# Sliding-window attention and two MLPs: S as an fp32 product of unsplit q and k

## The chip, the cores and the metric

The kernel runs on one core of a Trainium2 chip. The metric is the device time of one execution in microseconds; of the kernel before there are three, with a median of 708.91 us (707.36 to 709.56). The core has five engines with an instruction queue each, worked off in program order: PE (matmul), DVE, ACT, POOL and SP, which here only issues transfers.

## The reference

```python
def _attn_ref(q, k, v, n_global, n_local):       # 2 batches, 8 heads, 768 rows, 64 wide
    scores = (1 / np.sqrt(D)) * np.matmul(q, k.transpose(0, 1, 3, 2))
    keep = is_global | is_local                  # first 8 columns, or the last 96 positions
    bias = -slopes[:, None, None] * dist[None, :, :]
    scores = np.where(keep, scores + bias[None], -1e9)
    a = np.exp(scores - np.max(scores, axis=-1, keepdims=True))
    a = a / (np.sum(a, axis=-1, keepdims=True) + 1e-09)
    return np.matmul(a, v)
def _moe_ref(x, w_gate, w_val, w_out, rms_g):    # 1536 tokens, 512 wide, 1536 inside
    rms = np.sqrt(np.mean(x * x, axis=-1, keepdims=True) + 1e-06)
    xn = x / rms * rms_g
    g = xn @ w_gate
    return (g / (1 + np.exp(-g)) * (xn @ w_val)) @ w_out
def _moe2_ref(x, w_in, w_out, s, b):             # 2048 inside
    r = np.maximum(x @ w_in, 0.0)
    return (s * (r * r) + b) @ w_out
```

The output is `_moe2_ref(_moe_ref(attention))`. The weights come as 8-byte floats, q, k and v as fp32. The fast program, the one that runs here, covers the case of 8 global columns and 96 local ones.

## The kernel before, in words

The attention is cut into 12 units of 128 query rows: units 0 and 1 are the first rows of the two batches (128 key columns), units 2 to 6 and 7 to 11 the others (232 columns: 8 global ones, 96 earlier, 128 own). A unit is worked in two groups of four heads. For each group: the score products S on PE; the bias added and the minimum taken on DVE (`top`); exponentials on ACT; the sum inverted on DVE; the normalisation (`nrm`) on POOL or DVE; transposes P on PE; a copy from PSUM (`cp`); the product X with v on PE. After both groups the unit's RMS norm (`finish`): squares, their sum over 512 features, a mean through PE (L377), the root on POOL, a broadcast through PE (L388), a scaling, and the split of x into a high and a low half in the reduced format `float32r`.

Products of fp32 numbers in `float32r` are made in three terms (high x high, low x high, high x low). q and k are split for that too: `q_hi` and `k_hi` (a rounding copy on ACT or DVE, L759 and L761, L781 and L783) and `q_lo` and `k_lo` (a subtraction, L764 and L787). q is loaded into one raw buffer and k into another; the split writes into a persistent window of k (`kw`, three slots of 136 columns) and a pair of buffers of q.

Beside the attention run the first weights: 512 KB loads into three raw buffers, and seven steps of conversion from 8-byte floats into two halves (`conv`: ACT, four or five on DVE, POOL). Gate and value products of the first MLP are put between the attention's products as soon as their inputs are there (`gate`: 256 columns, three terms). The rest of both MLPs follows as a dense row of matmuls of 512 columns; two more conversions and loads run ahead of it all the time.

The order on every engine comes from `arrange`, a list scheduler that runs while the program is built. Each operation has a kind, a rank, durations on the engines that may do it, and resources (buffers) that it takes and gives back; `AHEAD` shifts the rank of a kind. A transfer counts there as an issue on SP plus a fixed delay. SP issues loads strictly in the order found; `lq`, `lk`, `lv` and `wload` are their kinds. PE gets idle matmuls (`warm`) in planned gaps of the first 40 us.

Of the kernel before, what the change touches and what calls it, by code (L numbers as in the profile page):

```python
# [8 lines left out]
F32 = mybir.dt.float32  # L9
# [31 lines left out]
    "P": -8.16, "S": -6.41, "X": 42.13, "bias": 20.72, "bias0": -89.67, "conv": 2.49, "cp": -19.31, "exp": -0.05,  # L41
    "fin": -19.74, "gate": -44.51, "inv": -11.3, "lk": -17.92, "lq": -12.18, "lv": -13.03, "mask": 103.87, "nrm": 110.41,
    "silu": -12.26, "split": -0.02, "top": -12.96, "wload": -16.57,
}
CONV = 1.65

SPARE = {"V": 0.95, "A": 0, "P": 0}
LOOK = {"V": 0.01, "A": 0.21, "P": 0.23, "T": 0}
KEEP = 3
COLD = 40.0  # L50
# [4 lines left out]
def kernel(  # L55
# [131 lines left out]
    class Mlp:  # L187
# [171 lines left out]
        def finish(self, nrm, xb, b, c0):  # L359
# [235 lines left out]

    class Op:
        def __init__(self, kind, rank, fn, on, after=(), take=(), give=()):
            self.kind, self.fn, self.on, self.after, self.take, self.give = kind, fn, on, after, take, give
            self.rank = rank + AHEAD.get(kind, 0.0)
            self.item = None  # L600
            self.start = self.end = self.eng = None


    def arrange(ops, size):
        free = dict.fromkeys("PVATS", 0.0)
# [3 lines left out]
        while left:  # L609
            cands = []  # L610
            for op in left:
# [19 lines left out]
                _, d, e, t = min((max(t, free[e]) + d + SPARE.get(e, 0.0), d, e, max(t, free[e])) for e, d in op.on.items())  # L631
                cands.append((t, op, d, e))
# [4 lines left out]
            free[e] = end  # L637
            for r in op.take:
                takes[r].append(op)
# [6 lines left out]
    def fast_program(fctx):  # L646
# [8 lines left out]
        in_p = pool("in_p", 1)  # L655
        v_p = pool("v_p", 2)
        qs_p = pool("qs_p", 2)
# [6 lines left out]
        size = {"xx": 1, "u": 2, "yy": 1, "w": 2, "qraw": 1, "kraw": 1, "v": 2, "qs": 2, "kw": 1, "kf": 1, "t": 3, "pt": 2}  # L664
# [3 lines left out]
        def op(kind, rank, fn, on, after=(), take=(), give=()):  # L668
            ops.append(Op(kind, rank, fn, on, after, take, give))
            return ops[-1]  # L670

# [5 lines left out]
        def bias_of(e, hs):  # L677
# [3 lines left out]
        bias0 = op("bias0", 0.6, bm0_half, {"V": 0.55})  # L681
        masked = op("mask", 3.0, lambda e: mask(D1, scr, PREV), {"V": 1.1})
        biases = [
            op("bias", 3.1 + g, lambda e, g=g: bias_of(e, range(4 * g, 4 * g + 4)), {"V": 0.8, "P": 3.6}, [masked]) for g in range(2)
# [4 lines left out]
        for n in range(RING):  # L689
            r = 3.0 + CONV * n  # L690
            if n < 3:
                loads[n] = op("wload", -3 + 0.1 * n, lambda e: mlp.load(), {"S": 0.9}, take=["raw"])
# [8 lines left out]
            lag = 2.5 if n else 4.0  # L701
            a = a0 = op("conv", r, begin, {"A": 0.7}, [(loads[n], lag)], ["cv"])
            for m, on in enumerate(({"V": 0.45}, {"V": 0.5}, {"V": 0.7}, {"V": 0.7}, {"A": 0.64}, {"V": 0.72, "P": 1.45}), 1):
                a = op("conv", r, lambda e, part=part, m=m: part[m](e), on, [a], give=[("raw", loads[n])] * (m == 4) + [("cv", a0)] * (m == 6))
                if m == 4 and n + 3 < RING:

                    loads[n + 3] = op("wload", r, lambda e: None, {"S": 0.9}, [a], ["raw"])
            convs.append(a)


        xs, kbuf, owner = [], {}, {}
        for n, (b, i) in enumerate(units):
# [5 lines left out]

            if n:

                def load_q(e, st=st, b=b, i=i):
                    st["q"] = in_p.tile([128, NPAIR, 128], F32, name="q", tag="q")
                    nc.sync.dma_start(st["q"], q[b, i])


                slot = 0 if i <= 1 else (i - 1) % 3 if b else i % 3
                if b == 0:
                    slot = i % 3
                fresh = not first and slot == 0
                kw_cols = 128 if first else WIN if fresh else KB  # L730

                def load_k(e, st=st, b=b, i=i, first=first, w=kw_cols):
                    kt = in_p.tile([128, NPAIR, WIN], F32, name="k", tag="k")
                    st["k"] = kt[:, :, WIN - w :]
                    if w == WIN:
                        nc.sync.dma_start(kt[:, :, :PREV], k[b, i - 1, :, :, KB - PREV :])
                    nc.sync.dma_start(kt[:, :, WIN - min(w, KB) :], k[b, i, :, :, GLOB * first :])

                lq = op("lq", r - 4, load_q, {"S": 0.45}, take=["qraw"])
                lk = op("lk", r - 4, load_k, {"S": 0.45}, take=["kraw"])  # L740
                lag = 2.2
            else:
                st["q"], st["k"] = q0, k0
                slot, fresh, kw_cols = 0, False, 128
                lq = lk = op("lq", -9, lambda e: None, {"S": 0.1}, take=["qraw", "kraw"])
                lag = 0.0
# [6 lines left out]
            lv = op("lv", r - 3.5, load_v, {"S": 0.6}, take=["v"])  # L753

            def q_hi(e, st=st):
                st["qh"] = qs_p.tile([128, NPAIR, 128], F32R, name="qhi", tag="qhi")
                st["ql"] = qs_p.tile([128, NPAIR, 128], F32R, name="qlo", tag="qlo")
                if e is V:
                    V.tensor_copy(st["qh"], st["q"])  # L759
                else:  # L760
                    A.activation(st["qh"], st["q"], AF.Copy)  # L761

            def q_lo(e, st=st):
                e.tensor_tensor(st["ql"], st["q"], st["qh"].bitcast(F32), op=ALU.subtract)  # L764

            def k_hi(e, st=st, n=n, b=b, i=i, slot=slot, fresh=fresh, w=kw_cols):
                first = i == 0
                if first and b:

                    kb = [bm_p.tile([128, NPAIR, 128], F32R, name=f"kf{m}") for m in range(2)]  # L770
                    st["w"] = kb
                    dst = kb
                else:
                    if first or fresh:
                        kbuf[b] = [bm_p.tile([128, NPAIR, PREV + 3 * KB], F32R, name=f"kw{m}", tag=f"kw{m}") for m in range(2)]
                    c1 = PREV + (slot + 1) * KB
                    dst = [t[:, :, c1 - w : c1] for t in kbuf[b]]
                    st["w"] = [t[:, :, c1 - (128 if first else WIN) : c1] for t in kbuf[b]]
                st["kd"] = dst
                if e is V:  # L780
                    V.tensor_copy(dst[0], st["k"])  # L781
                else:
                    A.activation(dst[0], st["k"], AF.Copy)  # L783

            def k_lo(e, st=st):
                hi, lo = st["kd"]
                e.tensor_tensor(lo, st["k"], hi.bitcast(F32), op=ALU.subtract)  # L787

            wide = NPAIR * kw_cols
            new = ["kf"] if first and b else ["kw"] if (first or fresh) else []  # L790
            qh = op("split", r - 1.5, q_hi, {"A": 0.63, "V": 0.5}, [(lq, lag)], ["qs"])
            ql = op("split", r - 1.5, q_lo, {"V": 0.72, "P": 1.35}, [qh], give=[("qraw", lq)])
            kh = op("split", r - 1.5, k_hi, {"A": 0.2 + 0.00084 * wide, "V": 0.2 + 0.0006 * wide}, [(lk, lag)], new)
            kl = op("split", r - 1.5, k_lo, {"V": 0.16 + 0.00105 * wide, "P": 0.9 + 0.0011 * wide}, [kh], give=[("kraw", lk)])
            if new:
                owner[new[0]] = kh
            own = "kf" if first and b else "kw"
            last_use = (first and b) or n + 1 == NU or (b == 0 and i in (2, 5)) or (b == 1 and i == 3)
            X = []
            for g in range(2):  # L800
# [344 lines left out]
```

## Time and profile before

| | |
|---|---|
| runs, median (range) | 708.91 us (707.36 to 709.56) |
| profiled execution | 707.75 us, span 706.0 us |
| PE busy | 663.3 us (94%) |
| DVE busy | 436.5 us (62%) |
| ACT busy | 286.2 us (41%) |
| POOL busy | 183.3 us (26%) |
| chain that ended last | PE 78%, DVE 9%, DMA 6% |

Shares over the whole span mix two parts. Up to some 162 us the attention runs and all engines take part; behind it PE is busy nearly throughout. The busy time of PE is made of overlapping matmuls, so it says less than the chain of waits, which gives each matmul only its place in the row. A wait that ends with a load of q is a stretch in which the chain's next instruction had nothing but that load to wait for.

### The profile page before, as it was taken

Reading aid. Unit: us, or ns where it says so; the run is one execution under the profiler, and the core shown is the slowest. Engines: PE = TensorE matmul, PEld = TensorE weight load, DVE = VectorE, ACT = ScalarE, POOL = GpSimd, SP = SyncE. Lnnn points to the kernel's source line nnn. Section 1 sums busy time; section 2 is a strip of 40 time slices with the busy share of each in tenths; the row PEclk is TensorE's granted clock in tenths of the full one; section 3 lists DMA queues with packets and bytes.
Section 4 is the critical chain, followed back from the end, with each engine's and each line's share of the span. In section 5 each row is a group of like instructions: output and inputs, shape, how many; then the busy total and the mean of one; then the engine's idle time right before and its main releaser. Section 6 shows DMA issues by size and latency. Waiting matters only on the chain.

```text
span 706.0 us, 9562 instructions
## 1 busy us (share of the span) xinstructions
PE 663.3 (94%) x3558; PEld 549.5 (78%) x3558; DVE 436.5 (62%) x879; ACT 286.2 (41%) x599; POOL 183.3 (26%) x153
## 2 busy tenths in 40 slices
PE   7667959899999999999999999999999997999996
PEld 5456858798888888888888887888888875888885
DVE  5877859963775555777532379766565699322322
ACT  3576748771332222334332335333333444322321
POOL 2467658751221111222200023221111124000000
PEclk9889889999999999999999999999999999999999
DMA  5444244400232222333300024222212233100101
GB/s 179 112 122 143 60 131 128 133 30 1 65 114 64 83 64 60 94 110 96 90 1 0 1 61 120 89 89 61 60 59 64 81 95 90 61 1 0 60 0 65
DMA packets 40334, 51.82 MB, mean 73 GB/s; under 512 B 4424, under 2 KB 31048, under 8 KB 40280
## 3 DMA queue, kind: packets, MB, share of 16 engines
q1 hardware_dynamic: 39608, 50.87, 24.2%
q8 instruction: 30, 0.49, 0.3%
q10 hardware_dynamic: 672, 0.26, 0.1%
q14 instruction: 24, 0.20, 0.1%
HBM read 47.98 MB, written 3.15 MB: 72 GB/s over the span
## 4 chain that ended last, share of the span: by engine, by line
PE 78%; DVE 9%; DMA 6%; ACT 2%; issue 2%; POOL 1%; SPq 1%; ACTq 0%; DVEq 0%; POOLq 0%
PE ps L182 24%; PE ps L184 24%; PE ps L183 24%; DMA q<-in_q_dram 5%; PE ps L884 2%; DVE u L269 2%; DVE u L275 2%; PE ps L810 1%; PE ps L865 1%; DVE t L823 1%; DVE u L272 1%; DMA words<-in_n_local_dram 1%; DVE sm L844 1%; DVE u L266 1%; ACT t L838 1%
## 5 line engine op out<-in xcount | busy, mean ns | idle before, releaser
L182 PE MATMUL ps<-xyh,hi_i 128*128 128x512 f32 x192 | 74.7, 389 | 0.0
L183 PE MATMUL ps<-xyl,hi_i 128*128 128x512 f32 x192 | 74.7, 389 | 0.0
L184 PE MATMUL ps<-xyh,lo_i 128*128 128x512 f32 x192 | 74.7, 389 | 0.0
L182 PE MATMUL ps<-xyh,hi_g 128*128 128x512 f32 (+1 forms) x176 | 63.0, 358 | 0.9 <-DVE p L949 0.9
L182 PE MATMUL ps<-xyh,hi_v 128*128 128x512 f32 (+1 forms) x176 | 63.3, 360 | 0.3 <-ACT ss L394 0.3
L523 DVE SCALAR_TENSOR_TENSOR gt<-side,sb 128x512 f32<-128x512 f32 x48 | 37.6, 784 | 39.7 <-ACT side L522 39.7
L183 PE MATMUL ps<-xyl,hi_v 128*128 128x512 f32 (+1 forms) x176 | 61.8, 351 | 0.0
L183 PE MATMUL ps<-xyl,hi_g 128*128 128x512 f32 (+1 forms) x176 | 61.7, 350 | 0.0
L184 PE MATMUL ps<-xyh,lo_v 128*128 128x512 f32 (+1 forms) x176 | 61.6, 350 | 0.0
L184 PE MATMUL ps<-xyh,lo_g 128*128 128x512 f32 (+1 forms) x176 | 61.6, 350 | 0.0
L522 ACT ACTIVATE side<-ps 128x512 f32<-128x512 f32 x48 | 28.7, 598 | 76.5 <-PE ps L184 76.5
L288 POOL TENSOR_TENSOR lo_i<-u,hi_i 128x512 fp32r<-128x512 f32 x16 | 23.3, 1455 | 138.9 <-ACT hi_i L284 137.5
L435 ACT ACTIVATE side<-ps 128x512 f32<-128x512 f32 (+1 forms) x32 | 18.3, 571 | 95.8 <-PE ps L184 95.8
L269 DVE TENSOR_SCALAR u<-u 128x512 int32<-128x512 int32 x68 | 51.2, 753 | 0.0
L838 ACT ACTIVATE t<-t,mn 128x232 f32<-128x232 f32 (+1 forms) x96 | 44.2, 463 | 15.9 <-DVE mn L823 15.9
L436 DVE SCALAR_TENSOR_TENSOR side<-side,ps 128x512 f32<-128x512 f32 (+1 forms) x32 | 20.9, 654 | 42.8 <-ACT side L435 42.8
L266 DVE TENSOR_SCALAR u<-u 128x512 f32<-128x512 f32 x68 | 40.2, 593 | 4.6 <-ACT u L262 4.5
L183 PEld LDWEIGHTS ps<-xyl,hi_i 128*128 128x128 f32 x192 | 36.0, 188 | 7.6
L184 PEld LDWEIGHTS ps<-xyh,lo_i 128*128 128x128 f32 x192 | 36.0, 188 | 7.5
L182 PEld LDWEIGHTS ps<-xyh,hi_i 128*128 128x128 f32 x192 | 36.0, 188 | 7.4
L884 PE MATMUL ps<-pt,vw 116*64 116x128 f32 (+1 forms) x352 | 27.2, 300 | 14.8 <-ACT pt L872 12.5
L288 POOL TENSOR_TENSOR lo_p<-u,hi_p 128x512 fp32r<-128x512 f32 x16 | 22.0, 1377 | 72.4 <-ACT hi_p L284 67.6
(155 smaller groups left out, 1654.7 us busy)
## 6 DMA issues: line engine op xcount, KB each, us to landing
raw_i<-in_moe_w_in_dram SPq DMA_DIRECT2D x16, 512.0 KB, 3.6
raw_p<-in_moe_w_out_dram SPq DMA_DIRECT2D x16, 512.0 KB, 3.6
raw_g<-in_moe_w_gate_dram SPq DMA_DIRECT2D x12, 512.0 KB, 3.6
raw_v<-in_moe_w_val_dram SPq DMA_DIRECT2D x12, 512.0 KB, 6.6
raw_o<-in_moe_w_out_dram SPq DMA_DIRECT2D x12, 512.0 KB, 3.4
vw<-in_v_dram SPq DMA_DIRECT2D x10, 464.0 KB
out_dram<-o SPq DMA_DIRECT2D x12, 256.0 KB, 2.9
q<-in_q_dram SPq DMA_DIRECT2D x11, 256.0 KB, 4.1
```

The lines of the kernel that those rows point to most:

```text
L182: T.matmul(out=o, lhsT=ahi, rhs=bhi, start=first, stop=False)
L183: T.matmul(out=o, lhsT=ahi, rhs=blo, start=False, stop=False)
L184: T.matmul(out=o, lhsT=alo, rhs=bhi, start=False, stop=last)
L266: e.tensor_scalar(u, u, 2.0**-15, None, op0=ALU.max)
L269: V.tensor_scalar(ui, ui, 5, 2, op0=ALU.logical_shift_left, op1=ALU.logical_shift_right)
L288: e.tensor_tensor(lo, u, hi.bitcast(F32), op=ALU.subtract)
L435: A.activation(th[:, :w], g, AF.Tanh, scale=0.5)
L436: V.scalar_tensor_tensor(th[:, :w], in0=th[:, :w], scalar=1.0, in1=g, op0=ALU.add, op1=ALU.mult)
L522: A.activation(r, o, AF.Relu)
L523: V.scalar_tensor_tensor(g, in0=r, scalar=s_col, in1=r, op0=ALU.mult, op1=ALU.mult)
L838: A.activation(t[:, hh, :], t[:, hh, :], AF.Exp, bias=mn[:, hh : hh + 1], scale=-1.0, accum_out=sm[:, hh : hh + 1])
L884: T.matmul(out=st["xb"][64 * j : 64 * j + 64, (2 * g + pp) * 128 : (2 * g + pp + 1) * 128], lhsT=st["v"][:kn, m, (4 * g + hh) * D : (4 * g ...
```

## The change

S is one fp32 product of q and k as they were loaded; the 24 splits of the units are gone, and the buffers for them. q is loaded into one of three buffers, k straight into its slot of the window, which is a resource of its own for the scheduler. The scheduler gets an engine `D` on which transfers take their size over 220 KB/us, and a port: an operation on POOL and one on DVE that is marked `port` do not overlap in the plan. In units 0 to 3 (`SUMMED`) the sum of squares over the four feature blocks is made by four products into one PSUM column, without the adds on POOL or DVE. The table `AHEAD`, `CONV`, `SPARE` and `LOOK` have new values. Of a gate and value pair both weights must be converted before the gate product starts.

```diff
 AHEAD = {
-    "P": -8.16, "S": -6.41, "X": 42.13, "bias": 20.72, "bias0": -89.67, "conv": 2.49, "cp": -19.31, "exp": -0.05,
+    "P": -44.35, "S": 19.7, "X": 23.57, "bias": 26.48, "bias0": -17.44, "conv": 1.04, "cp": -65.5, "exp": -1.83,
...
+RATE = 220.0
+SUMMED = 4
...
             def total(e):
                 part["R"] = ps("w")
-                T.matmul(out=part["R"][:, 128:129], lhsT=ss, rhs=ones, start=True, stop=True)
+                parts = [xn[:, kk] for kk in range(KD)] if summed else [ss]
+                for kk, x in enumerate(parts):
+                    T.matmul(out=part["R"][:, 128:129], lhsT=x, rhs=ones, start=kk == 0, stop=x is parts[-1])
...
+                for e, d in op.on.items():
+                    s = max(t, free[e])
+                    if e == "P" or e == "V" and op.port:
+                        s = max(s, port["V" if e == "P" else "P"])
+                    key = (s + d + SPARE.get(e, 0.0), d, e, s)
+                    best = key if best is None else min(best, key)
...
-        size = {"xx": 1, "u": 2, "yy": 1, "w": 2, "qraw": 1, "kraw": 1, "v": 2, "qs": 2, "kw": 1, "kf": 1, "t": 3, "pt": 2}
+        size = {"xx": 1, "u": 2, "yy": 1, "w": 2, "v": 2, "q": 3, "k0": 1, "k1": 1, "k2": 1, "kf": 1, "t": 3, "pt": 2}
...
+        def fetch(kind, rank, fn, kb, after=(), take=(), issue=0.45):
+            a = op(kind, rank, fn, {"S": issue}, after, take)
+            return a, (op(kind, rank, None, {"D": kb / RATE}, [a]), 1.8)
...
+            c1 = PREV + (slot + 1) * KB
+            st["k"] = k0 if n == 0 else kalone if first else kwin[:, :, c1 - WIN : c1]
+
+            def load_q(e, st=st, b=b, i=i):
+                st["q"] = qs_p.tile([128, NPAIR, 128], F32, name="q", tag="q")
+                nc.sync.dma_start(st["q"], q[b, i])
+
+            def load_k(e, st=st, b=b, i=i, first=first, fresh=fresh):
+                if fresh:
+                    nc.sync.dma_start(st["k"][:, :, :PREV], k[b, i - 1, :, :, KB - PREV :])
+                nc.sync.dma_start(st["k"][:, :, 0 if first else PREV :], k[b, i, :, :, GLOB * first :])
...
+                gone = ["kf"] if first else [f"k{m}" for m in range(3) if m == slot - 1 or m == slot and (m == 2 or i == NT - 1)]
+                gone = [("q", lq)] + [(x, user[x]) for x in gone]
...
-                        for m, (qq, kk) in enumerate((("qh", 0), ("ql", 0), ("qh", 1))):
-                            for j in range(2):
-                                T.matmul(
-                                    out=st["sc", g][:, j, pp, :],
-                                    lhsT=st[qq][64 * j : 64 * j + 64, pr, :],
-                                    rhs=st["w"][kk][64 * j : 64 * j + 64, pr, :],
-                                    start=m == 0,
-                                    stop=m == 2,
-                                )
+                        for j in range(2):
+                            T.matmul(
+                                out=st["sc", g][:, j, pp, :],
+                                lhsT=st["q"][64 * j : 64 * j + 64, pr, :],
+                                rhs=st["k"][64 * j : 64 * j + 64, pr, :],
+                                start=True,
+                                stop=True,
+                            )
...
-            a = ga = op("gate", rf, lambda e, p=product, st=st: p(e, st, "g", 0), {"T": 0.74}, xdep + [convs[2 * f]] + hold, ["w"])
+            a = ga = op("gate", rf, lambda e, p=product, st=st: p(e, st, "g", 0), {"T": 0.74}, xdep + [convs[2 * f], convs[2 * f + 1]] + hold, ["w"])
```

SP from the start of the fast program. Before: weights (`raw_g`, `raw_v`), then k, v and q of units 1 and 2.

```order
L237 DMA raw_g<-in_moe_w_gate_dram 128x4x256
L237 DMA raw_v<-in_moe_w_val_dram 128x4x256
L237 DMA raw_g<-in_moe_w_gate_dram 128x4x256
L737 DMA k<-in_k_dram 128x4x128
L751 DMA vw<-in_v_dram 128x512 x2
L723 DMA q<-in_q_dram 128x512
L737 DMA k<-in_k_dram 128x4x136
L723 DMA q<-in_q_dram 128x512
L737 DMA k<-in_k_dram 128x4x136
```

And now (`kf` is unit 1's k, `kw` the window):

```order
L770 DMA vw<-in_v_dram 128x512
L239 DMA raw_g<-in_moe_w_gate_dram 128x4x256
L239 DMA raw_v<-in_moe_w_val_dram 128x4x256
L239 DMA raw_g<-in_moe_w_gate_dram 128x4x256
L752 DMA kf<-in_k_dram 128x4x128
L747 DMA q<-in_q_dram 128x512
L770 DMA vw<-in_v_dram 128x512
L751 DMA kw<-in_k_dram 128x4x96
L752 DMA kw<-in_k_dram 128x4x136
L747 DMA q<-in_q_dram 128x512
L752 DMA kw<-in_k_dram 128x4x136
L747 DMA q<-in_q_dram 128x512
```

The v of unit 0 stands first, and the loads of q and k reach unit 3 before the first weight that must wait for a raw buffer; before, a weight and a v stood ahead of unit 3's q.

SP in the second half, where unit 7's window starts again in the first slot (the two `kw` rows of 96 and 136 columns). Before, from the k of unit 7 (L736, L737) on:

```order
L736 DMA k<-in_k_dram 128x4x96
L737 DMA k<-in_k_dram 128x4x136
L751 DMA vw<-in_v_dram 116x2x512
L237 DMA raw_g<-in_moe_w_gate_dram 128x4x256
L751 DMA vw<-in_v_dram 116x2x512
L723 DMA q<-in_q_dram 128x512
L737 DMA k<-in_k_dram 128x4x136
L723 DMA q<-in_q_dram 128x512
L237 DMA raw_v<-in_moe_w_val_dram 128x4x256
```

And now:

```order
L239 DMA raw_v<-in_moe_w_val_dram 128x4x256
L239 DMA raw_g<-in_moe_w_gate_dram 128x4x256
L239 DMA raw_v<-in_moe_w_val_dram 128x4x256
L770 DMA vw<-in_v_dram 116x2x512
L751 DMA kw<-in_k_dram 128x4x96
L752 DMA kw<-in_k_dram 128x4x136
L239 DMA raw_g<-in_moe_w_gate_dram 128x4x256
L752 DMA kw<-in_k_dram 128x4x136
L747 DMA q<-in_q_dram 128x512
```

The loads of k of unit 7 now stand behind three weights and a v, and q of units 7 and 8 is already ahead of them.

PE at unit 2, the first with 232 columns. Before, its second group: S in six rows of two matmuls (`qhi`, `qlo`; `kw_214` and `kw_215` are the halves of k), then transposes and X of earlier groups.

```order
L377 MATMUL ps_470<-ones,ss 128x1
L810 MATMUL ps_474<-kw_214,qhi 128x232 x2
L810 MATMUL ps_474<-kw_214,qlo 128x232 x2
L810 MATMUL ps_474<-kw_215,qhi 128x232 x2
L810 MATMUL ps_474<-kw_214,qhi 128x232 x2
L810 MATMUL ps_474<-kw_214,qlo 128x232 x2
L810 MATMUL ps_474<-kw_215,qhi 128x232 x2
L865 MATMUL ps_491<-ident,t 128x128 x4
L388 MATMUL ps_470<-ident,rstd 128x128
L884 MATMUL ps_513<-pt,vw 64x128 x4
L865 MATMUL ps_519<-ident,t 128x128 x4
```

And now, from its first group on:

```order
L783 MATMUL ps_418<-kw,q 128x232 x4
L835 MATMUL ps_424<-ident,t 128x128 x4
L176 MATMUL ps_446<-warm 128x512 x3
L854 MATMUL ps_450<-pt,vw 64x128 x4
L783 MATMUL ps_455<-kw,q 128x232 x4
L176 MATMUL ps_477<-warm 128x512 x5
L835 MATMUL ps_483<-ident,t 128x128 x4
L783 MATMUL ps_490<-kw,q 128x232 x4
L854 MATMUL ps_450<-pt,vw 64x128 x4
```

S is one row of four matmuls; the idle matmuls (`warm`) stand in other places.

## Rows read from the trace of the kernel before

**Rows 1.** Stretches: us, then PE, PEld, DVE, ACT, POOL busy, PEclk, DMA share, GB/s
```profile
8.00:162.20 154.20, 126.53 (x1155) 107.64 (x1156) 122.39 (x396) 100.88 (x291) 98.32 (x81) 0.90 0.39 115
162.20:706.00 543.80, 532.57 (x2395) 438.71 (x2393) 310.79 (x462) 183.48 (x306) 83.56 (x61) 1.00 0.21 62
```

**Rows 2.** Chain of waits to 165 us: start us, us, what
```profile
27.83 9.62 DMA q<-in_q_dram
57.84 7.01 DMA q<-in_q_dram
87.90 9.25 DMA q<-in_q_dram
127.42 4.12 DMA q<-in_q_dram
162.02 0.22 PE ps L388 x2
```

**Rows 3.** Stretches: sum over the four waits of rows 2; then 110 to 140
```profile
sum 30.00, PE 19.60 PEld 16.42 DVE 20.73 ACT 10.40 POOL 16.73; mean PE 4.90 PEld 4.11 DVE 5.18 ACT 2.60 POOL 4.18
110.00:140.00 30.00, 27.23 (x290) 24.55 (x290) 29.37 (x89) 24.34 (x68) 24.24 (x21) 1.00 0.46 143
```

**Rows 4.** Timeline of SyncE, 78 to 88 us: start, us, what
```profile
78.45 0.28 SPq L751 DMA_DIRECT2D vw<-in_v_dram  x1
86.91 0.39 SPq L237 DMA_DIRECT2D raw_g<-in_moe_w_gate_dram  x1
87.90 0.41 SPq L723 DMA_DIRECT2D q<-in_q_dram  x1
```

**Rows 5.** Stretch, lines 787, 764 (DVE, POOL busy), 759, 781 (DVE busy)
```profile
8.00:162.20 154.20, 8.09 (x6) 8.89 (x6) 0.90 0.39 115
8.00:162.20 154.20, 0.75 (x1) 15.87 (x11) 0.90 0.39 115
8.00:162.20 154.20, 2.36 (x5) 0.90 0.39 115
8.00:162.20 154.20, 0.83 (x2) 0.90 0.39 115
```

**Rows 6.** Groups of DVE, 8 to 162.2 us: busy, mean ns, idle before
```profile
L849 DVE TENSOR_TENSOR t<-t,sm 128x928 f32<-128x928 f32 (+1 forms) x5 | 6.4, 1287 | 0.1
L413 DVE TENSOR_TENSOR xyl<-xn,xyh 128x512 fp32r<-128x512 f32 x3 | 2.3, 774 | 0.7 <-ACT xyh L409 0.7
L870 DVE COPY pt<-ps 116x1024 f32<-116x1024 f32 x2 | 2.4, 1224 | 1.7 <-PE ps L865 1.7
L373 DVE TENSOR_REDUCE ss<-xn 128x128 f32<-128x512 f32 x2 | 2.1, 1064 | 0.0
L844 DVE TENSOR_SCALAR sm<-sm 128x4 f32<-128x4 f32 x24 | 12.1, 503 | 0.6 <-ACT t L838 0.5
```

**Rows 7.** Chain of waits, 140 to 165 us, pieces of PE: start, us, what
```profile
144.97 0.12 PE ps L182
145.33 0.86 PE ps L810 x12
146.19 1.02 PE ps L884 x16
148.12 0.22 PE ps L388 x2
150.99 0.87 PE ps L865 x8
```

**Rows 8.** Timeline: DVE L844, POOL L849, DVE L272 beside it, and alone
```profile
78.28 0.17 DVE L844 TENSOR_SCALAR sm<-sm 128x4 f32<-128x4 f32 x1
87.22 2.58 POOL L849 TENSOR_TENSOR t<-t,sm 128x928 f32<-128x928 f32 x1
88.13 2.21 DVE L272 SCALAR_TENSOR_TENSOR u<-raw_g,u 128x512 int32<-128x512 int32 x1
420.17 0.69 DVE L272 SCALAR_TENSOR_TENSOR u<-raw_i,u 128x512 int32<-128x512 int32 x1
```

More of the change, by code (lines that the diff above doesn't have):

```diff
@@ L596, with __init__ @@
     class Op:
-        def __init__(self, kind, rank, fn, on, after=(), take=(), give=()):
+        def __init__(self, kind, rank, fn, on, after=(), take=(), give=(), port=False):
             self.kind, self.fn, self.on, self.after, self.take, self.give = kind, fn, on, after, take, give
+            self.port = port
             self.rank = rank + AHEAD.get(kind, 0.0)
@@ L604, in arrange @@
     def arrange(ops, size):
-        free = dict.fromkeys("PVATS", 0.0)
+        free = dict.fromkeys("PVATSD", 0.0)
+        port = {"P": 0.0, "V": 0.0}
         takes = {r: [] for r in size}
@@ L630, in arrange @@
                     continue
-                _, d, e, t = min((max(t, free[e]) + d + SPARE.get(e, 0.0), d, e, max(t, free[e])) for e, d in op.on.items())
-                cands.append((t, op, d, e))
+                best = None
+                for e, d in op.on.items():
[4 more added lines that the diff above has]
+                    best = key if best is None else min(best, key)
+                cands.append((best[3], op, best[1], best[2]))
             t0, _, _, e = min(cands, key=lambda c: (c[0], c[1].rank))
@@ L637, in arrange @@
             free[e] = end
+            if e == "P" or e == "V" and op.port:
+                port[e] = end
             for r in op.take:
@@ L691, in fast_program @@
             if n < 3:
-                loads[n] = op("wload", -3 + 0.1 * n, lambda e: mlp.load(), {"S": 0.9}, take=["raw"])
+                loads[n] = fetch("wload", -3 + 0.1 * n, lambda e: mlp.load(), 512, take=["raw"])
             part = []
@@ L699, in begin @@
                 part[0](e)
-            lag = 2.5 if n else 4.0
-            a = a0 = op("conv", r, begin, {"A": 0.7}, [(loads[n], lag)], ["cv"])
+            a = a0 = op("conv", r, begin, {"A": 0.7}, [loads[n][1]], ["cv"])
             for m, on in enumerate(({"V": 0.45}, {"V": 0.5}, {"V": 0.7}, {"V": 0.7}, {"A": 0.64}, {"V": 0.72, "P": 1.45}), 1):
-                a = op("conv", r, lambda e, part=part, m=m: part[m](e), on, [a], give=[("raw", loads[n])] * (m == 4) + [("cv", a0)] * (m == 6))
+                a = op("conv", r, lambda e, part=part, m=m: part[m](e), on, [a], give=[("raw", loads[n][0])] * (m == 4) + [("cv", a0)] * (m == 6), port=True)
                 if m == 4 and n + 3 < RING:
-                    loads[n + 3] = op("wload", r, lambda e: None, {"S": 0.9}, [a], ["raw"])
+                    loads[n + 3] = fetch("wload", r, lambda e: None, 512, [a], ["raw"])
             convs.append(a)
-        xs, kbuf, owner = [], {}, {}
+        xs, user = [], {}
         for n, (b, i) in enumerate(units):
@@ L717, in fast_program @@
             st = {}
-            if n:
[L721 to L741, printed above, removed]
-            else:
[L743 to L746, printed above, removed]
@@ new lines, in fast_program @@
+            slot = (i - 1) % 3
+            fresh = not first and slot == 0
+            if n == 0:
+                kwin = bm_p.tile([128, NPAIR, PREV + 3 * KB], F32, name="kw")
+                kalone = bm_p.tile([128, NPAIR, 128], F32, name="kf")
+            c1 = PREV + (slot + 1) * KB
[3 more added lines that the diff above has]
+                nc.sync.dma_start(st["q"], q[b, i])
@@ new lines, in load_k @@
+            def load_k(e, st=st, b=b, i=i, first=first, fresh=fresh):
+                if fresh:
+                    nc.sync.dma_start(st["k"][:, :, :PREV], k[b, i - 1, :, :, KB - PREV :])
+                nc.sync.dma_start(st["k"][:, :, 0 if first else PREV :], k[b, i, :, :, GLOB * first :])
+            gone = []
+            if n:
+                place = "kf" if first else f"k{slot}"
+                lq, lqd = fetch("lq", r - 4, load_q, 256, take=["q"])
+                lk, lkd = fetch("lk", r - 4, load_k, 464 if fresh else 272, take=[place], issue=1.0 if fresh else 0.45)
+                have = [lqd, lkd]
+                user[place] = lk
+                gone = ["kf"] if first else [f"k{m}" for m in range(3) if m == slot - 1 or m == slot and (m == 2 or i == NT - 1)]
+                gone = [("q", lq)] + [(x, user[x]) for x in gone]
+            else:
+                st["q"], have = q0, []
@@ L763, in q_lo @@
[L763 to L798, printed above, removed]
+            lv, lvd = fetch("lv", r - 3.5, load_v, kn * nm * 2, take=["v"])
             X = []
@@ L849, in normalise @@
                     e.tensor_tensor(t, t, st["sm", g].unsqueeze(2).to_broadcast([128, 4, W]), op=ALU.mult)
-                s_ = op(
-                    "S", rg, scores, {"T": 0.75}, [ql, kl], ["xx"],
-                    ([("qs", qh)] + [(own, owner[own])] * bool(last_use)) if g else [],
-                )
+                s_ = op("S", rg, scores, {"T": 0.55 if first else 0.9}, have, ["xx"], gone if g else [])
                 bdep = ([bias0] if g else []) if first else [biases[g]]
@@ L893, in fast_program @@
                     op(
-                        "X", rg, apply, {"T": 0.55 if first else 1.0}, [cp, (lv, 2.5)], [] if g else ["u"],
+                        "X", rg, apply, {"T": 0.55 if first else 1.0}, [cp, lvd] + X, [] if g else ["u"],
                         [("pt", cp)] + [("v", lv)] * g,
@@ L913, in fast_program @@
                         "fin", r + 1.2, lambda e, m=m, stage=stage: stage(e, m=m), on, a,
-                        ["nr"] * (m == 0) + ["w"] * (m == 2), give,
+                        ["nr"] * (m == 0) + ["w"] * (m == 2), give, port=m > 7,
                     )
@@ L973, in fast_program @@
             if o.item in late:
+                continue
+            if o.eng == "D":
                 continue
```

48 lines of the change are left out of this document (22 added, 26 removed).

## The prediction

> **What bounds the kernel now.** I read the table of stretches first, then the chain of waits, the SyncE timeline, the groups by shape, and last the timeline around single instructions. Between 8 and 162.2 us PE is busy for 126.5 of 154.2 us, behind that for 532.6 of 543.8 [rows 1]. At 162.2 us the last norm broadcast (L388) ends [rows 2]; what follows is matrix work of the two MLPs. The change leaves the late part as it is, so its price is read from the stretch 8 to 162.2 us, called the stage.
>
> In the stage no engine is full, DVE is nearest: 122.4 us busy, 31.8 idle [rows 1]. The chain of waits names the load of q four times behind the first 20 us: 9.62, 7.01, 9.25 and 4.12 us, 30.0 together [rows 2]. During these DVE was not wholly idle: the four stretches hold 20.7 us of its work, so only 9.3 us of idling [rows 3]. In others it is the bound: 29.4 of 30 us between 110 and 140 [rows 3]. Both must shrink for the stage to shrink.
>
> Why the loads are late is seen on SyncE, which issues in program order. At 78.45 a load of v goes out; the next issue, of weights, follows at 86.91, since it waits for a free raw buffer; v and q queue behind it and q leaves at 87.90 [rows 4]. The chain then waits 9.25 us for it [rows 2]. By the code that wait ends at an ACT or DVE instruction, the one that makes the high half of q, and what is queued behind it there, such as the copy of P for the next product, waits as well.
>
> **The change part by part.** *Splits.* On DVE they cost 8.1 us (low halves of k), 0.75 (one low half of q), 2.4 and 0.8 (high halves): 12.0 us; on POOL 8.9 + 15.9 = 24.8 us [rows 5]. All go, with the high halves that ACT made.
>
> *What the freed POOL takes over.* By the order, all 24 normalisations and all 12 low halves of the normed x now stand on POOL, both double copies of P go to ACT, and no sum of squares is left on DVE. That takes 6.4 + 2.3 + 2.4 + 2.1 = 13.2 us from DVE [rows 6]; one rounding of x and one copy of the broadcast come to it, some 0.8 us by the rounding of q, 2.36 us for five [rows 5]. DVE's work falls by 12.0 + 13.2 - 0.8 = 24.4 us, to 98.0. POOL loses the 24.8 us and two of its ten sums of squares, and gains some 11 us.
>
> *Loads.* q has three buffers instead of one and k goes straight to its window, so a load is issued one to two units ahead and no ACT or DVE instruction waits for it; the matmul does. SyncE still issues in order, with weights among the q loads. I take the 9.3 us of idling as gone. Bounds: none of it is saved, or all and the 20.7 us are worked off elsewhere (they are in the 98.0 already). The wait for unit 1's q in the first 20 us stays: 2.3 MB are still ahead of or with it.
>
> *A new wait.* A k slot is free only once the score products of its last user are done; formerly the raw buffer let the transfer run early. It shows at unit 7, whose k (464 KB in two transfers) waits for unit 6's products. On PE stand 24 gate matmuls and 24 matmuls and transposes of unit 5 between the two (some 5 us by the pieces in [rows 7]), and the load took 4.1 us from issue in the quickest of the old stalls [rows 2]. Behind the waiting matmul stand unit 7's other products and the gates, and DVE and ACT wait for those. I take 3 us; bounds 0 and 9.3, the longest old stall.
>
> *S in fp32.* The trace has no fp32 product with 64 rows. The nearest row has 64 columns: the 16 records (8 products) of P with v, 128 columns wide, take 1.02 us, two of them side by side; so a pair of records takes 0.11 us at 128 columns and, scaled, 0.20 at 232. The new S has 4 products, 8 records, 4 pairs: 0.79, with the 0.15 that X too has over its 8 pairs' 0.87, 0.94 us, against 0.86 now [rows 7]. Over 20 groups that is +1.6. Lower bound 0.79 (nothing above the stream: -1.4 in all), upper 1.7 (pairs not side by side: +18). I take 0.94, as the row is of the same data type and differs only in which half of the array is shared. The sum of squares of units 0 to 3 costs three more fp32 products each, about 0.6 us by the 0.22 for the two records of one product [rows 7], 2.6 us; in return the adds on POOL leave its chain. PE works longer by some 4 us, of which I put 3 on the path, since it is the last to be served in the second half.
>
> *Gates.* In front of the last norm broadcast stand 270 gate matmuls instead of 246. At 0.12 us [rows 7] 2.9 us move ahead of that point and leave the part behind it: nothing in the sum. What covers them is PE's waiting between attention groups; if that is gone, the stage grows by what the rest loses.
>
> *Planner.* Due times, port rule and look-ahead cost nothing by themselves; their effect is the order, counted above.
>
> *The sum.* 154.2 - 24.4 (DVE's work) - 9.3 (its idling) + 3 (slot of k) + 3 (PE) = 126.5 us, so the last broadcast ends near 134.5 instead of 162.2. As a check on PE: its rows give 20 x (0.94 + 0.87 + 1.02), the small groups and norms, and 270 x 0.12, about 104 us, so 22 of the 126 us may be idle or cold; before it was about 98 of 154. Behind lie 543.8 - 2.9 = 540.9 us. Span 675.4. The profiled execution took 707.75 us for a span of 706.0, and the median of the runs is 708.91: the latter 2.9 more than the span. That gives 678 us for the median, 31 less.
>
> **A rule weighed.** At 87.22 a normalisation on POOL takes 2.58 us, and the DVE instruction started at 88.13 beside it takes 2.21, where the same operation takes 0.69 alone [rows 8]. So work on POOL delays DVE, and 8.7 us of DVE's work now goes to POOL. The Trainium skill, SBUF — State Buffer, section "SBUF: two separate sides", says that the two share a port pair under an exclusive lock and that whoever comes second waits for the whole instruction, also where DVE has two SBUF inputs. By that the two engines' SBUF work may not overlap anywhere: POOL's 98.3 - 24.8 + 11 us [rows 1, 5] and DVE's conversions and inversions, by an estimate 31 us, make 115 in a row, a stage of about 122 and 674 us; this is no bound for the sum above, but it would rule out the fastest case below.
>
> **Rivals.**
> A. Packed tighter. L844 takes 0.17 us with POOL idle and 0.50 in the mean [rows 6, 8]; if the port rule in the planner takes most of such waits away (24 x 0.33 = 8, as much again on weights), the stage falls by another 16 us: 662. For it: DVE is 98% busy in the best old stretch [rows 3]. Against: PE's 104 us leave little room.
> B. Loads late again. A weight load waiting on SyncE ahead of q is still there. If two waits of 7 to 9 us come back on the path, 694; if all four do, with the k wait, the change gives back its 30 and is lost in no change. For it: the old stalls began at that queue. Against: three q slots.
> C. The fp32 pairs do not run side by side: +18 us on PE, some 14 on the path: 692.
> D. Slower. The 64-row fp32 products each run alone and at half clock, 8 x 0.40 us, twice the 0.20: 3.2 a group, +2.3 x 20 + 4 = 50 us on PE, which becomes the bound at 8 + 154 + about 18 idle: 180 us for the broadcast and 724 in all. It decides from about 2.4 us a group. Against it speaks the 1.02 us of 16 fp32 records; for it only that no row shows 64 rows.
> E. The change does not do what it says, the products wait for something else as long: 704 to 710.
>
> **How the numbers follow.** Forecast 0.57, by itself 668 to 690; A 0.17; B 0.12 (a quarter of it without a change); C 0.06; D 0.06; E 0.02. Within 0.3% (2.1 us, about what a measurement can tell) lie E and part of B: 0.04; slower is D and a hundredth of the rest: 0.07; faster 0.89. The range 660 to 697 takes in A, C and most of B; D, E and the tails, some 0.17, are left out.
>
> **What would show it.** Right: no wait for a q load over 3 us on the chain behind 25 us; S groups of 0.9 to 1.0 us; DVE near 98 us busy in the stage; last L392 (as it is numbered then) at 130 to 140 us; the part behind it 541 us. Wrong: S groups at 1.7 (C) or 3.2 (D); PE waiting over 5 us at the product of unit 7 or 10; a part behind the stage that is longer by more than 3 us, as then something in the MLPs moved that I hold fixed.

## The result and the profile after

The changed kernel takes 691.0 us (median of 4 runs, 689.02 to 692.54) against 708.13 us (706.27 to 709.56) before: a ratio of 0.976, with a 95% interval of 0.972 to 0.980. That is 17 us less. The forecast was 678, 31 less; the range held the time, the point did not. The direction is as forecast, the gain a little over half of it.

First the stretches: the stage up to the last norm broadcast (L392 now), the part behind it, and four short stretches that matter below. The columns are those of [rows 1].

```profile
8.00:146.70 138.70, 127.99 (x1104) 108.18 (x1105) 83.89 (x374) 94.22 (x276) 75.20 (x68) 0.94 0.46 130
146.70:688.00 541.30, 530.01 (x2370) 435.86 (x2369) 310.91 (x460) 182.99 (x304) 82.71 (x61) 1.00 0.21 62
52.90:56.80 3.90, 0.14 (x3) 0.02 (x1) 0.00 (x0) 0.83 (x2) 0.06 (x1) 0.84 0.42 135
56.80:62.30 5.50, 5.50 (x26) 5.50 (x27) 3.22 (x12) 1.86 (x3) 1.27 (x1) 0.50 0.14 52
83.90:88.00 4.10, 0.03 (x2) 0.06 (x2) 0.18 (x2) 1.00 (x1) 3.84 (x3) 0.79 0.81 185
88.00:93.00 5.00, 5.00 (x30) 4.14 (x30) 1.72 (x10) 2.00 (x8) 0.00 (x0) 0.50 0.13 41
```

The part behind takes 541.3 us, where 540.9 was forecast: the whole miss lies in the stage, which takes 138.7 us instead of 126.5. Against [rows 1] the stage is 15.5 us shorter, yet DVE's work in it fell by 38.5 us, from 122.4 to 83.9. So DVE no longer limits it. PE is nearest now, busy for 128.0 of 138.7 us; 12.6 of these are idle matmuls (`warm`), all before 40 us, and behind 40 us it is busy for 98.0 of 106.7 us without any. Twice PE stands still for about 4 us, and each time it then works at half clock (1.2 GHz, granted clock 0.50) for some 5 us.

What it stood still for is in the chain of waits: start, us, what. The first piece is around 50 us, the second around 80.

```profile
45.46 1.30 ACT t L811 x5
46.76 9.05 DMA raw_g<-in_moe_w_gate_dram
...
55.90 0.66 ACT u L264
56.56 0.18 ACT ss L398
...
56.78 0.58 PE ps L184
57.36 0.21 PE ps L185
...
76.82 0.98 PE ps L783 x8
...
77.84 9.99 DMA kw<-in_k_dram
87.83 0.14 issue
87.97 1.92 PE ps L783 x8
```

No load of q is left on the chain behind 8 us, where [rows 2] had four; nor is the load of unit 1's q, which was on the old chain at 11.42 us for 6.58 us and which the prediction took as staying. Two other loads are there, of 9.05 and 9.99 us. The first is the seventh weight: the conversion that reads it (L264) stands on ACT ahead of the copy of a norm broadcast (L398), for which PE's matmuls wait. The second is k of unit 7, the wait that the prediction called the slot of k; PE's products of that unit wait for it directly. Behind each the same matmul pieces are longer: 0.21 instead of 0.12 for a gate matmul, 1.92 instead of 0.98 for a group of S.

SyncE's timeline shows how k got there (start, us, what; compare [rows 4]):

```profile
71.14 0.37 SPq L239 DMA_DIRECT2D raw_v<-in_moe_w_val_dram  x1
76.89 0.28 SPq L770 DMA_DIRECT2D vw<-in_v_dram  x1
77.22 0.55 SPq L751 DMA_DIRECT2D kw<-in_k_dram  x1
77.84 0.59 SPq L752 DMA_DIRECT2D kw<-in_k_dram  x1
78.60 2.11 SPq L239 DMA_DIRECT2D raw_g<-in_moe_w_gate_dram  x1
80.76 2.24 SPq L752 DMA_DIRECT2D kw<-in_k_dram  x1
```

SyncE issues nothing for five microseconds, since v of unit 6 waits for a buffer. The first load of k, into columns that unit 6 doesn't read, goes out right behind that v at 77.22. The second waits until the last S of unit 6 is done, which by the chain above ends at 77.80, and lands 9.99 us after its issue. So the queue behind v and the slot hold k for almost equally long.

### The profile page after: what moved, and what is told of

It reads as the page before. It is cut to its first block, busy times and chain, and to the rows that moved or that the text cites. A ratio compares the mean times of both kernels' runs of the same rounds, so it can differ in the third digit from the quotient of the medians.

```text
span 688.0 us, 9365 instructions
## 1 busy us (share of the span) xinstructions
PE 662.2 (96%) x3482; PEld 547.1 (80%) x3482; DVE 398.2 (58%) x855; ACT 278.7 (41%) x582; POOL 159.3 (23%) x140
## 4 chain that ended last, share of the span: by engine, by line
PE 88%; DMA 4%; DVE 4%; ACT 3%; issue 1%; ACTq 0%; SPq 0%; DVEq 0%
PE ps L184 26%; PE ps L186 26%; PE ps L185 26%; PE ps L854 3%; PE ps L783 3%; PE ps L835 3%; DMA kw<-in_k_dram 1%; DMA raw_g<-in_moe_w_gate_dram 1%; ACT t L811 1%; PE ps L176 1%; DVE u L271 1%; DMA words<-in_n_local_dram 1%; DVE u L277 1%; ACT pt L842 1%; DMA raw_p<-in_moe_w_out_dram 1%
## 5 line engine op out<-in xcount | busy, mean ns | idle before, releaser
L439 ACT ACTIVATE side<-ps 128x512 f32<-128x512 f32 (+1 forms) x30 | 17.5, 585 | 92.0 <-PE ps L186 92.0
L822 POOL TENSOR_TENSOR t<-t,sm 128x928 f32<-128x928 f32 (+1 forms) x24 | 39.5, 1646 | 44.3 <-DVE sm L818 25.5
L271 DVE TENSOR_SCALAR u<-u 128x512 int32<-128x512 int32 x68 | 47.8, 702 | 0.0
L184 PEld LDWEIGHTS ps<-xyh,hi_g 128*128 128x128 f32 x176 | 33.9, 193 | 11.3 <-ACT ss L398 4.0
L268 DVE TENSOR_SCALAR u<-u 128x512 f32<-128x512 f32 x68 | 38.7, 571 | 5.1 <-ACT u L264 5.1
```

Of the source, the lines that this page charges most:

```text
L184: T.matmul(out=o, lhsT=ahi, rhs=bhi, start=first, stop=False)
L268: e.tensor_scalar(u, u, 2.0**-15, None, op0=ALU.max)
L271: V.tensor_scalar(ui, ui, 5, 2, op0=ALU.logical_shift_left, op1=ALU.logical_shift_right)
L822: e.tensor_tensor(t, t, st["sm", g].unsqueeze(2).to_broadcast([128, 4, W]), op=ALU.mult)
```

## The experiments

Theory 1, formed from this trace: the stage is longer than forecast because of these two loads, each with slow matmuls behind it; without them the forecast would nearly hold. The rivals: PE is limited elsewhere as well and other waits take their place; or the sum itself is wrong, in the splits, the loads of q, or the planner's part. Where an edit changes nothing in the plan, the instructions of all engines keep their order. All ratios are to the kernel before, run beside it on the same chip.

**E1, k of unit 7 early.** Batch 1 gets a k window of its own, and the load is issued ahead of v of unit 6 (`named` keeps the planned loads by unit):

```
+ kwin1 = bm_p.tile([128, NPAIR, PREV + 3 * KB], F32, name="kw1")
- ... kalone if first else kwin[:, :, c1 - WIN : c1]
+ ... kalone if first else (kwin1 if b else kwin)[:, :, c1 - WIN : c1]
+ plan.remove(named["k", 7])
+ plan.insert(plan.index(named["v", 6]), named["k", 7])
```

> The changed kernel, with a second window of k for batch 1, and the k of unit 7 issued ahead of the v of unit 6 instead of behind two scores of unit 6; nothing else moves. Theory 1 (the stage is 12 us longer than forecast because of two waits for loads, each with TensorE at half clock behind it): the wait of 9.99 us for the k of unit 7 leaves the chain, TensorE's idle 4.07 us at 83.9 goes, and so does the half clock to 93; the last broadcast at about 140.5 instead of 146.7, the kernel at 684 to 685 us (0.967 of before). Rival (TensorE's queue is limited elsewhere, so another wait of VectorE or ScalarE ends there): the idle time turns up at another matmul before 100 us, and the time stays within 2 us of 691.

Measured: 683.91 us, ratio 0.965 (0.962 to 0.969). The stretch of the stage, that from 75 to 95, and SyncE's timeline:

```profile
8.00:141.10 133.10, 126.98 (x1104) 106.84 (x1105) 83.60 (x374) 94.06 (x277) 75.43 (x68) 0.97 0.49 135
75.00:95.00 20.00, 20.00 (x191) 17.61 (x191) 13.14 (x68) 16.26 (x48) 13.98 (x12) 1.00 0.55 135
```
```profile
72.49 0.55 SPq L752 DMA_DIRECT2D kw<-in_k_dram  x1
73.08 0.63 SPq L753 DMA_DIRECT2D kw<-in_k_dram  x1
```

Issued 4.8 us earlier, the load costs nothing: PE is busy for 20 of 20 us at full clock. It also lands faster, 5.63 us after its issue. The kernel gains 7.1 us, of which 4.1 are the wait; of the rest, some 2.5 are what 5.0 us at half clock lose. Theory 1 holds, the rival of another wait falls. The edit takes away the slot and the place behind v together; either alone was not tried.

**E2, the seventh weight early.** It gets a tile of its own and is issued ahead of k of unit 6; the conversion that used to issue it issues nothing:

```
- r = self.raw.tile([128, 1024], I32, name=f"raw_{kind}", tag="raw")
+ r = self.own if self.loaded == 6 and self.own else self.raw.tile(...)
...
+ mlp.skip = mlp.seq[3:4]
+ if o is named["k", 6]:
+     mlp.load()
```

> The changed kernel, with a place of its own for the seventh weight, whose load is issued ahead of the k of unit 6 (about 43 us) instead of at 46.76 behind the fourth conversion; nothing else moves. Theory 1: ScalarE's wait of 4.2 us at L264 goes, the square sums behind it on ScalarE come in time, TensorE's idle 3.76 us at 53 and the half clock to 62 go; the last broadcast at about 140.5, the kernel at 684 to 685 us. Rival (the queue is so full at 43 us that the load lands no earlier, or the loads of q and k now land late in its place): a wait of like length at another load, 690 to 694 us.

Measured: 684.69 us, ratio 0.967 (0.963 to 0.971). The last broadcast ends at 140.9 and the wait for k is still there, as it should be:

```profile
40.97 12.59 DMA raw_g<-in_moe_w_gate_dram
...
73.08 9.81 DMA kw<-in_k_dram
```

The weight is issued 5.8 us earlier and takes 3.5 us longer to land, so it is still on the chain; PE now waits 1.4 us behind it instead of 3.8, and the granted clock from 50 to 62 us is 1.00 instead of 0.73. Theory 1 holds here too: 6.3 us.

**E3, both.**

> Both edits together: the k of unit 7 into a window of its own and early, the seventh weight into a place of its own and early. Theory 1: the two gains add, no load on the chain behind 40 us, TensorE at full clock from about 45 to the end of the stage, the last broadcast at 134 to 136, the kernel at 678 to 680 us (0.958 of before). Rival (either gain is a gain of the same slack): no better than the better one of the two alone, 684 to 688.

Measured: 680.08 us (678.5 to 681.02), ratio 0.959 (0.955 to 0.962): the fastest kernel of this study, faster than both. The stage, and the stretch 50 to 62 us, where the changed kernel had a granted clock of 0.73:

```profile
8.00:137.70 129.70, 125.43 (x1103) 105.20 (x1104) 83.56 (x374) 93.99 (x276) 75.45 (x68) 0.99 0.50 139
50.00:62.00 12.00, 11.07 (x102) 10.13 (x98) 8.29 (x35) 8.43 (x26) 6.28 (x5) 1.00 0.54 150
```

The gains nearly add: 10.9 us of 7.1 + 6.3. The stage takes 129.7 us, 3 more than the forecast of 126.5, which had 3 us for the slot of k that this kernel does not have: so 6 more than the rest of that sum. PE is busy for 125.4 of them, 14.1 with idle matmuls, again all before 40 us. Behind 40 us:

```profile
40.00:137.70 97.70, 95.36 (x906) 83.00 (x905) 60.02 (x259) 71.23 (x197) 60.18 (x57) 1.00 0.40 109
```

There, at full clock and without idle matmuls, what is left is PE's own work. Between 8 and 40 us PE's own work fills only half of the time (30.1 us busy less the 14.1); what holds that part was not tried.

**E4, one place for q.**

```
- qs_p = pool("qs_p", 3)
+ qs_p = pool("qs_p", 1)
- size = {... "q": 3, ...}
+ size = {... "q": 1, ...}
```

> The changed kernel with one place for q instead of three, so that a q is issued only behind the last scores of the unit before, as in the kernel before; the planner counts with it. It takes the early loads back and leaves the fp32 scores and the missing splits. By the prediction's sum (24.4 us from VectorE, 9.3 from the loads): the load waits come back, one per unit for which TensorE has little else, 7 to 9 us each before 60 us, and the kernel stands at 698 to 706 us. Rival (the splits alone carry the gain, the loads were hidden or wait anyway): 689 to 694 us, like the changed kernel.

Measured: 691.0 us, ratio 0.975 (0.971 to 0.978), the changed kernel's own time. My expectation failed and the rival's time came. The planner, told of the single place, made another order, and in that order PE waits elsewhere:

```profile
PE ps L783 <- issue: 7.1, 3, 4.2
PE ps L783 <- DVE D L107: 2.2, 1, 2.2
```

PE waits 7.1 us in three places for S, and the profile names no releaser. By the issue times they look like loads again: 4.25 us end at the first S of unit 2, whose q went out only at 23.47, behind the S of unit 1, and 2.56 at the first S of unit 7, whose k and q went out at 79.97 and 81.27. With 0.8 us more for a q that the profile does name, that is as much as PE's two pauses in the changed kernel (3.8 and 4.1 us); the wait for the seventh weight is gone. So waits of S for its loads did come back, and the time is the same as other waits left. The two orders differ throughout, so what three places for q are worth by themselves is not shown.

**E5, the splits back.** The 48 split instructions are done again, into tiles that nothing reads; S stays fp32, and the planner counts with them and puts S behind them (`h` for the high halves, `l` for the low):

```
+ h = op("split", r - 1.5, hi, {"A": 0.2 + 0.00084 * wide, "V": 0.2 + 0.0006 * wide}, have, [...])
+ return [op("split", r - 1.5, lo, {"V": 0.16 + 0.00105 * wide, "P": 0.9 + 0.0011 * wide}, [h], ..., port=True)]
```

> The changed kernel with the four split instructions of every unit done again (48 in all, into tiles that nothing reads, behind the loads and ahead of the planner's scores); S stays fp32, the loads stay early, the planner counts with the added work. By the prediction's sum the splits on VectorE (12.0 us) and what they push back onto it are worth up to 24 us: 703 to 712 us. Theory 1 as the trace of the changed kernel now has it (TensorE sets the end of the stage, VectorE idles some 55 us of 139): the splits fit into idle time except at the start of the stage, 693 to 699 us.

Measured: 712.93 us, ratio 1.006 (1.004 to 1.008). The whole gain is gone, and a little more: 22 us over the changed kernel. The expectation that they fit into DVE's idle time falls.

**E6, three later weights held back.** The loads of the ninth to eleventh weight, which the stage doesn't use, go out behind v of unit 10:

```
+ mlp.skip = mlp.seq[5:8]
+ if o is named["v", 10]:
+     for _ in range(3):
+         mlp.load()
```

> The changed kernel with the loads of the ninth, tenth and eleventh weight held back until the v of unit 10 has been issued (they are used behind the stage); the k of unit 7 stays in its old place behind the scores of unit 6. If the k lands late because 2 MB are under way with it (the weight of 78.60 among them): landing in about 7 us instead of 9.99, TensorE's idle 4.07 us falls to about 1 and the half clock behind it goes, 685 to 688 us. If it is late because it can be issued only at 77.84: the wait and the time stay, 690 to 692 us.

Measured: 691.59 us (686.11 to 692.59), ratio 0.974 (0.969 to 0.978): no difference. The k of unit 7 was issued at 80.84 in this run and took as long:

```profile
49.51 9.21 DMA raw_g<-in_moe_w_gate_dram
...
80.84 9.64 DMA kw<-in_k_dram
```

Half a megabyte less beside it changes 9.99 to 9.64, so the company of that weight is not what made it late. In E1 the same load landed 9.1 us earlier: 4.8 of them by the earlier issue and 4.4 by a shorter transfer (5.63 us). What the v, the other k and the q around it add was not tried apart.

**E7, no rule of the shared port in the planner.** `port=False` for every operation, and no wait for the other engine in `arrange`.

> The changed kernel with the planner's rule of the shared port taken out (VectorE and GpSimd may be planned side by side in all operations), everything else the same; the order of the whole stage is planned anew. Theory 1 (VectorE is not what sets the end): VectorE's busy time in the stage rises from 83.9 towards the 98.0 of the prediction, GpSimd's products take longer than 1646 ns in the mean, and the time moves by less than 5 us, 688 to 696 us. Rival (the rule carries a good part of the gain): 698 to 704 us.

Measured: 687.48 us, ratio 0.971 (0.969 to 0.973), not slower than the changed kernel (the intervals overlap). Its stage:

```profile
8.00:138.80 130.80, 123.22 (x1060) 101.51 (x1061) 95.08 (x378) 92.61 (x273) 70.19 (x59) 0.95 0.49 137
```

DVE's work is 95.1 us, close to the 98.0 of the prediction, so with the rule DVE has some 11 us less to do. Without it the stage is even shorter, 130.8 us, but it holds 49 gate matmuls fewer, and the part behind is 5 us longer. What DVE gains from the rule carries no time in these two orders.

**E8, the sums of squares as before** (`SUMMED = 0`).

> The changed kernel with the sums of squares of the first four units done as those of the later ones (by VectorE or GpSimd, one product with the ones instead of four). By the prediction this takes some 1 to 3 us from TensorE in the first 60 us and gives them to VectorE or GpSimd: 689 to 693 us, no difference. Rival (the additions were what the chain waited for at the start): 695 us or more.

Measured: 692.94 us, ratio 0.978 (0.976 to 0.980): no difference, as expected. DVE's work in the stage is 90.8 us.

**E9, the splits in the finished order.** E5 mixes the splits' work with a new order. Here the same 48 instructions on the same engines are put into the changed kernel's own order, at the time at which the planner has the transfer end. That is 1.8 us ahead of the time from which it counts the data as there, so the splits stand a little early:

```
+ a.start = min(load.end if load else 9.0, limit)
+ z.start = min(a.start + 1.0, limit)
+ plan += [a, z]
+ plan.sort(key=lambda o: o.start)
```

> The changed kernel with the same 48 split instructions on the same engines as in e5 (20 on VectorE, 15 on ScalarE, 13 on GpSimd), put into the finished order when the planner expects their data, all else in the order of the changed kernel. If their work itself costs what e5 lost: 706 to 713 us. If e5 lost it by the new order that the planner made with them: 692 to 700 us.

Measured: 718.67 us, ratio 1.016 (1.010 to 1.022): it was not the new order. The chain shows what else there is:

```profile
43.89 7.87 DMA kw<-in_k_dram
...
51.87 0.07 ACT kh L781
...
56.88 3.86 DMA kw<-in_k_dram
...
60.83 0.44 DVE kh L779
...
67.49 6.61 DMA q<-in_q_dram
...
74.12 0.64 ACT qh L781
...
93.58 9.77 DMA kw<-in_k_dram
...
103.43 0.98 ACT kh L781
```

With two more (4.71 and 8.81 us behind 110 us) there are six loads on the chain, 41.6 us together from issue to landing, and a split on ACT or DVE comes behind each. ACT and DVE stand idle for 23.8 us before such splits.

**E10, a planner for which transfers take no time.** `RATE = 1.0e6` instead of 220.

> The changed kernel with a planner for which a transfer's bytes take no time (1.8 us behind the issue everything has landed; RATE 1.0e6 instead of 220). If counting the transfers is a part of the gain, matmuls and conversions stand in the order ahead of their data and the waits for loads on TensorE grow by 4 to 10 us: 695 to 702 us. If it is not, 688 to 694 us.

Measured: 704.56 us, ratio 0.995 (0.993 to 0.998), 13.6 us slower than the changed kernel, a little beyond what I gave it. PE's three longest waits in the stretch 8 to 150 us (us in total, times, longest):

```profile
PE ps L835 <- POOL t L822: 9.8, 1, 9.8
PE ps L783 <- DMA kw<-in_k_dram: 4.8, 1, 4.8
PE ps L783 <- DMA q<-in_q_dram: 3.9, 1, 3.9
```

The wait of 9.8 us goes back to a load as well: on the chain ahead of it stands the seventh weight, 10.27 us from its issue at 43.25, then its conversion on ACT and DVE, and then the normalisation. So an order that does not count the transfers waits longer for them, as expected.

**E11, E3 in the order without the port's rule.**

> The edits of e3 (k of unit 7 and the seventh weight early) in the order that the planner makes without the rule of the shared port (as in e7). If the 3.5 us between e7 and the changed kernel are an order with less waiting for loads, nothing is left to add to e3: 679 to 683 us. If the rule itself costs time, 675 to 678 us.

Measured: 695.14 us, ratio 0.981 (0.976 to 0.985): slower than E7 and than E3, outside both expectations. Its chain has the seventh weight at another bad place:

```profile
46.65 12.37 DMA raw_g<-in_moe_w_gate_dram
...
59.10 0.04 ACT u L266
...
59.66 1.02 ACT pt L848
...
60.73 1.96 PE ps L841 x8
```

The conversion on ACT now stands ahead of a copy of P, and PE waits 3.8 us and then goes at half clock (1.96 us for a group of transposes). Here an edit made for one order was worth nothing in another. Whether the rule itself costs time stays open.

**E12, splits that never wait.** As E9, but the 48 instructions read a tile that is there from the start:

```
+ still = h_p.tile([128, NPAIR, WIN], F32, name="still")
- ... lambda st=st: st["q"] ...
+ ... lambda: still[:, :, :128] ...
```

> As e9, the same 48 split instructions on the same engines at the same places in the order, but reading a tile that is there from the start instead of q and k: the work stays, the waits for the loads go (the chain of e9 has six such waits of together 41.6 us). If a split costs by its work: 710 us or more, like e9 (718.7). If it costs by making VectorE and ScalarE, which take their work in order, wait for a load: 692 to 700 us.

Measured: 701.03 us, ratio 0.991 (0.989 to 0.993), just beyond the upper end of one expectation and far from the other. The stage:

```profile
8.00:158.10 150.10, 130.53 (x1104) 108.20 (x1104) 109.81 (x395) 102.67 (x291) 96.03 (x81) 0.98 0.42 120
```

So of the 27.7 us that the splits cost in this order, 10.0 are their work (the time over the changed kernel; 0.84 of it fills the tile) and 17.6 go when they no longer read q and k. The kernels ran on different chips; by the ratios it is 10.9 and 17.5. DVE has 25.9 us more to do in this stage than in the changed kernel's, and the stage is 11.4 us longer. The waits of ACT and DVE for a load are what the trace of E9 shows for the 17.6. A part may be that a place of k is freed later when a split reads it too, and a part that E9 sets the splits 1.8 us early; neither was tried apart.

## Why the prediction came out as it did

*What bounds the kernel.* The view of before was right in its parts (loads of q late on a queue that issues in order, the part behind fixed) and wrong in its measure. I took DVE's busy time as the length of the stage, term by term. DVE lost 38.5 us and the stage 15.5; and E7 gives DVE 11 us back at no cost. After the change PE is the bound behind 40 us (E3). Two of the signs of being right did not come: DVE near 98 us (it was 83.9) and the last L392 at 130 to 140 us (146.7).

*Splits, 24.4 us.* The size fits: putting them back costs 22 us (E5) to 27.7 (E9). That it fits is luck, since the reason given was the smaller half of it. Work alone is 10.0 us (E12), though DVE, ACT and POOL all have more of it there, DVE 25.9 us; so the 12.0 us of splits and the 13.2 us that moved from DVE to POOL are not the stage's microseconds. The rest goes with the reading of q and k: by the trace of E9 mostly because an engine that takes its work in order stops at a load. The prediction saw that wait, but in another term.

*Loads, 9.3 us.* The waits for q did go, but "I take the 9.3 us of idling as gone" failed as a saving of its own. The seventh weight came in their place (E2: 6.3 us), and E4 shows no net gain from the places for q as planned. Rival B came nearest: two long waits back on the path and 694 us, but for q. It named the weight on SyncE as a cause of late q loads; that the weight itself would come late, and stop ACT, was not seen.

*The slot of k, 3 us.* This is the mis-sized term. Unit and place were right, and so was the mechanism, but for the queue behind v, which held k almost as long. The wait of 4.07 us lay between the bounds of 0 and 9.3; but it cost 7.1 us (E1), since I had counted the wait alone and not the half clock behind it. The 4.1 us for the transfer was the least of the old waits, whereas it landed 9.99 us after its issue.

*S in fp32.* A group takes 0.98 us at full clock, where 0.94 was worked out: over 20 groups 0.8 us. Rivals C (1.7) and D (3.2) are out. The row with 64 columns was the right one to scale from.

*Sum of squares and gates.* E8 shows no difference, and the part behind the stage fell as forecast. The 24 gate matmuls that moved ahead, 2.9 us, were put at nothing as long as PE's waiting covers them; in E3 PE has 2.3 us without work left behind 40 us, where the kernel before had 17.5 in 122.2.

*The sum.* 691.0 - 678 leaves 13 us. The two loads cost 10.9 (E3), of which the forecast had 3 already; so they are some 8 of the 13. Of the 5 that stay, PE's own work is the likely holder: 111.3 us in the stage of E3 (125.4 less the idle matmuls), where the check by rows gave about 104, and the gates above are a part of it. This was not tried apart.

*The rule weighed.* The Trainium skill, SBUF — State Buffer, section "SBUF: two separate sides", has VectorE and GpSimd wait for one another at a shared port. The trace agrees that there is something to save: 83.9 us of DVE work in the stage with the planner keeping them apart, 95.1 without. It changed no time in these two orders, since DVE was not the bound; the 674 us worked out beside it did not come. Rival A had DVE's work fall by another 16 us: it did fall 14 below the 98.0, but the time that was to follow did not, for the same reason.

## What to carry to other kernels

The busy time of the busiest engine is a price for a stage only as long as nothing else takes over. Before summing savings, ask for each part of the stage what the next engine needs there: here PE, which with both loads early was busy for 95.4 of the 97.7 us behind 40 us. When an instruction that waits for a load is removed from an engine that works in order, price the work queued behind it, not the instruction: here, between E9 and E12, that was nearly twice the work. A wait on TensorE costs itself and the slow clock behind it, and after a change of buffers the next late load is found by following every load in the issue order, the weights too.

## What was not expected of the hardware

A transfer of 272 KB landed 9.99 us after its issue, with v, the other part of its k, a weight, another k and a q under way around it; without the weight it still took 9.64 (E6), and 5.63 when it was issued 4.8 us earlier, ahead of v (E1). Issued 5.8 us earlier, a load of 512 KB took 12.59 us instead of 9.05 (E2): here an earlier place gave back less than the time by which it was earlier, and in E1 it gave back more. And two pauses of PE of about 4 us were each followed by about 5 us at half clock, so that an edit gained 3.0 us (E1: 7.1 less 4.1) and 3.9 us (E2: 6.3 less 2.4) beyond the pause that it took away.
